# Decode attention with a DMA-bound cache stream: three more visits per layer turn with K as the moving operand, and loads into aligned slots

## The chip, the cores and the metric

One core of a Trainium2 chip. The metric is device time in microseconds (us) of the program, lower is better. The kernel before was measured at 2340.02 us (median of 3 runs, 2339.74 to 2343.99) when the prediction was made. The record sorts runs into a fast and a slow state by time and clock. Experiments 1 to 3 and the larger dose of experiment 4 ran on one chip, the others on a second one, each with runs of the kernel before in the same rounds.

Words used below. A *unit* is 512 KB of the K or V cache: 128 partitions, 4 KB each. A *visit* is the attention of one pair of heads of one batch row in one layer: four units of K, then four of V. *Batch row* b has 16 visits in layer 0 and 16 in layer 1. A *turn* is the place where the stream of visits goes from layer 0 to layer 1 of a row. There are eight. In the views, PE is TensorE's matmuls, PEld its weight loads, DVE is VectorE, ACT ScalarE, POOL GpSimd and SP SyncE, which issues the loads. In the traces each load of the cache has 16 completion records, and it *lands* when the last of them arrives. That each record stands for another of the 16 DMA engines of the page is my reading: the records do not name the engine.

## The reference, cut to what matters

```python
# B=8, Sq=1, D=640, 32 heads of 128, Sk=4096, Dff=1728; bf16
def _A_ref(x, k_cache, v_cache, wq, wo):
    q = (x @ wq) per head
    p = softmax(q @ k^T * Dh**-0.5)
    return (p @ v, heads joined) @ wo
x = x + _A_ref(_layernorm(x), A_k_cache, A_v_cache, A_wq, A_wo)
x = x + _B_ref(_layernorm(x), B_w1, B_w2)          # relu feed-forward
x = x + _A_ref(_layernorm(x), A_k_cache, A_v_cache, A_wq, A_wo)   # the same caches again
x = x + _B_ref(_layernorm(x), B_w1, B_w2)
```

Both layers read the same caches, 512 MB in all. What layer 1 can find on the chip need not be loaded again.

## The kernel before

A planner in Python writes one list of operations, and each engine gets its part in that order. The cache goes through an *arena* of 26 unit slots. At the end of layer 0 of a row, 21 slots keep units for layer 1 (three more wait outside the arena, in PSUM but for half a unit), so that only five slots take turns while the turn runs (the prediction's "24 of the 26" counts those three in):

```python
G = 26
SPARE = 5
...
keep = set(first[: G - SPARE])
stash = first[G - SPARE : G - SPARE + STASH]
```

Two visits of the next row ("ahead") are put in front of the first layer-1 visit, so that the feed-forward, the norm and the queries of the turn have something to hide behind. The visits that matter, with t the first visit of layer 1: t-3 is the last of layer 0, t-2 and t-1 are the two ahead.

K scores are formed in one of two ways. With K *still*, 16 blocks of 128x128 of a unit are loaded as weights and the query is one moving column. With K *moving*, the unit moves as four matmuls of 512 columns, and the score row must be turned again afterwards (PT, copied by PC):

```python
moving = [not any(t - AHEAD - 1 <= i < t + 5 for t in turns) and i < NV - 2 for i in range(NV)]
...
    for c in range(4):
        if moving[i]:
            nc.tensor.matmul(
                s_ps[32 * c : 32 * c + CJ, :], lhsT=qz[:, i % 3, c // 2, 3 - g : 3 - g + CJ],
                rhs=arena[:, at + c * BANK : at + (c + 1) * BANK], ...)
            continue
        ...
        for n in range(4 * c, 4 * c + 4):
            nc.tensor.matmul(s_tiles[i][:, j : j + 1], lhsT=arena[:, at + n * P : at + (n + 1) * P],
                             rhs=qo[:, b, h : h + 1], start=True, stop=True)
```

A load takes n neighbouring free units, up to 8, and goes where the slots have been free longest:

```python
def room(n):
    us = [u for u in range(G - n + 1) if not any(owner[u : u + n])]
    return min(us, key=lambda u: max(freed[u : u + n])) if us else None
```

In the turn the plan is a ring: consume a unit, release its slot, load one unit into it. For the second turn of the kernel before it reads (K-2.0 is unit 0 of K of visit t-2; `[ld1]` a load of one unit; T, M2, B, E are the steps of the softmax, C those of the feed-forward):

```
K-1.3 [ld1] M1 -1; C down 1; L -2; I -2
V-2.0 [ld1] C down 2; T -1; M2 -1
V-2.1 [ld1] C down 3; B -1; E -1
V-2.2 [ld1] C down 4; C add
V-2.3 [ld1] OC -2; L -1; I -1; C mean; C center
```

## Time and profile before

| | before |
|---|---|
| time | 2340.02 us |
| load queue, share of 16 DMA engines' span | 99.4% |
| PE busy | 60% |
| rate between turns, in turns (stretches of 20 us) | about 432, 370 to 415 GB/s |

From the page of the kernel before: its span, the rates in 40 slices, the load queue and the instruction fetches (packets, MB, share of 16 engines), and the chain of what ended last, by engine.

```profile
span 2343.0 us, 43024 instructions
...
GB/s 411 430 433 401 433 432 432 431 396 432 432 432 430 404 434 431 430 427 403 433 432 431 426 412 434 430 432 420 427 431 427 432 416 430 431 431 431 396 433 329
...
q1 hardware_dynamic: 76564, 988.12, 99.4%
q8 instruction: 146, 2.39, 0.4%
...
DMA 71%; PE 17%; ACT 6%; DVE 3%; issue 2%; SPq 0%; POOL 0%; ACTq 0%; DVEq 0%; POOLq 0%
```

The load queue is busy for the whole span. The rate stands near 430 except for a dip in every fifth slice or so: 401, 396, 404, 403, 412, 420, 416, 396. Those are the eight turns.

The groups of instructions that the change touches (line, engine, operation, out<-in, shapes, count; busy us, mean ns of one; idle before it and what ended that):

```profile
L695 PE MATMUL s_ps<-arena,qz 128*4 128x512 bf16 x3040 | 410.3, 602 | 261.1 <-DMA arena<-in_A_kv_dram 249.5
L713 DVE TENSOR_REDUCE mrow<-s_ps 100x1 bf16<-100x512 f32 x190 | 131.8, 694 | 323.2 <-PE s_ps L695 323.2
...
L705 PE MATMUL s_ps<-qo,arena 128*128 128x1 bf16 x3712 | 123.7, 165 | 17.2 <-ACT P_sb L761 7.6
L768 PE MATMUL small_ps<-few,P_row 100*128 100x16 bf16 x760 | 52.3, 179 | 92.1 <-ACT P_row L755 92.1
```

L695 is K moving, L705 K still. L713 (the maximum over the row, 0.69 us) and L768 (the turning of the row) exist for moving visits.

The loads of the cache, from the list of DMA issues (count, KB each, median us from issue to landing):

```profile
arena<-in_A_kv_dram SPq DMA_DIRECT2D x124, 4096.0 KB, 23.1
arena<-in_A_kv_dram SPq DMA_DIRECT2D x98, 2048.0 KB, 22.7
arena<-in_A_kv_dram SPq DMA_DIRECT2D x218, 512.0 KB, 6.5
arena<-in_A_kv_dram SPq DMA_DIRECT2D x48, 1024.0 KB, 11.3
```

The second turn in the view of stretches (start:end, us; busy us and count of PE, PEld, DVE, ACT, POOL; granted clock, DMA share, GB/s):

```profile
480.00:500.00 20.00, 15.92 (x385) 12.39 (x383) 4.91 (x29) 2.50 (x10) 2.33 (x11) 1.00 0.97 368
500.00:520.00 20.00, 16.16 (x341) 10.76 (x338) 5.18 (x30) 4.38 (x14) 2.54 (x12) 1.00 1.02 401
```

And PE in the timeline of the same turn (start us, length us, what; in brackets the idle time before it and what ended it). L687 are the V units, L580 is the down product of the feed-forward:

```profile
499.23 0.59 PE L687 MATMUL o_ps<-arena,P_sb 128*4 128x512 bf16 x4
499.76 0.62 PE L580 MATMUL small_ps<-hT,w_sb 128*128 128x1 bf16 x14
500.45 0.60 PE L687 MATMUL o_ps<-arena,P_sb 128*4 128x512 bf16 x4
500.99 0.23 PE L781 MATMUL s_ps<-P_sb,few 128*128 128x64 bf16 x1
501.53 0.19 PE L492 MATMUL s_ps<-s1h,few 128*128 128x1 bf16 x2 [0.32 <-DVE lsum L787]
501.74 0.59 PE L687 MATMUL o_ps<-arena,P_sb 128*4 128x512 bf16 x4
```

The V units follow each other at 499.23, 500.45 and 501.74: one per 1.2 to 1.3 us, the pace at which units land.

### The profile page before, as it was taken

How to read it: one execution, taken by the hardware profiler on the slowest of the kernel's cores; microseconds unless marked ns; L12 is line 12 of the kernel's file. 1: busy time of each engine (PE TensorE's matmuls, PEld its weight loads, DVE VectorE, ACT ScalarE, POOL GpSimd, SP SyncE). 2: the span in 40 equal slices, each digit the busy share in tenths (PEclk: the TensorE clock that was granted, in tenths of full speed). 3: DMA queues.
4: the chain of work that ended last, by engine and by line, in shares of the span. 5: the costliest groups of instructions: out<-in, count | busy, mean ns of one | idle time of the engine just before them, and what ended most of it. 6: DMA issues, size and time to landing. Idle time of an engine off the chain costs nothing.

```text
span 2343.0 us, 43024 instructions
## 1 busy us (share of the span) xinstructions
PE 1398.6 (60%) x18748; PEld 591.4 (25%) x18748; DVE 496.7 (21%) x2022; ACT 426.3 (18%) x986; POOL 59.5 (3%) x296
## 2 busy tenths in 40 slices
PE   3547654576545764557545675556755567545766
PEld 1214211152111511125111241113411133111523
DVE  1113211131112211122111221112211122111312
ACT  1111211122111221112211121111211112111211
POOL 0000000000000000000000000000000000000000
PEclk9999999999999998555555555555555555555555
DMA  9999999999999999999999999999999999999997
GB/s 411 430 433 401 433 432 432 431 396 432 432 432 430 404 434 431 430 427 403 433 432 431 426 412 434 430 432 420 427 431 427 432 416 430 431 431 431 396 433 329
DMA packets 76753, 990.87 MB, mean 423 GB/s; under 512 B 8596, under 2 KB 8596, under 8 KB 36500
## 3 DMA queue, kind: packets, MB, share of 16 engines
q1 hardware_dynamic: 76564, 988.12, 99.4%
q8 instruction: 146, 2.39, 0.4%
q14 instruction: 43, 0.35, 0.0%
HBM read 988.08 MB, written 0.01 MB: 422 GB/s over the span
## 4 chain that ended last, share of the span: by engine, by line
DMA 71%; PE 17%; ACT 6%; DVE 3%; issue 2%; SPq 0%; POOL 0%; ACTq 0%; DVEq 0%; POOLq 0%
DMA arena<-in_A_kv_dram 71%; PE o_ps L687 5%; PE s_ps L695 4%; PE s_ps L705 2%; ACT P_row L755 2%; ACT o_sb L795 1%; PE small_ps L655 1%; DVE mrow L713 1%; ACT P_sb L761 1%; PE small_ps L800 1%; ACT arena L634 1%; PE small_ps L768 1%; PE small_ps L825 1%; DVE hmx L732 0%; ACT nmax L753 0%
## 5 line engine op out<-in xcount | busy, mean ns | idle before, releaser
L687 PE MATMUL o_ps<-arena,P_sb 128*4 128x512 bf16 x3952 | 584.3, 596 | 402.0 <-DMA arena<-in_A_kv_dram 401.0
L695 PE MATMUL s_ps<-arena,qz 128*4 128x512 bf16 x3040 | 410.3, 602 | 261.1 <-DMA arena<-in_A_kv_dram 249.5
L687 PEld LDWEIGHTS <-P_sb 128*4 128x4 bf16 x3952 | 107.4, 88 | 502.8 <-issue 491.7
L713 DVE TENSOR_REDUCE mrow<-s_ps 100x1 bf16<-100x512 f32 x190 | 131.8, 694 | 323.2 <-PE s_ps L695 323.2
L795 ACT CAST o_sb<-o_ps 100x512 bf16<-100x512 f32 x247 | 144.9, 587 | 289.3 <-PE o_ps L687 286.0
L753 ACT ACTIVATE nmax<-small_ps 100x1 f32<-100x1 f32 x106 | 18.1, 171 | 774.5 <-PE small_ps L742 774.5
L775 DVE CAST P_sb<-small_ps 128x64 bf16<-128x64 f32 x190 | 42.6, 224 | 523.1 <-PE small_ps L768 523.1
L695 PEld LDWEIGHTS <-qz 128*4 128x4 bf16 x3040 | 63.9, 85 | 313.7 <-issue 295.5
L705 PEld LDWEIGHTS <-arena 128*128 128x128 bf16 x4224 | 129.6, 104 | 40.8 <-DMA arena<-in_A_kv_dram 23.4
L705 PE MATMUL s_ps<-qo,arena 128*128 128x1 bf16 x3712 | 123.7, 165 | 17.2 <-ACT P_sb L761 7.6
L768 PE MATMUL small_ps<-few,P_row 100*128 100x16 bf16 x760 | 52.3, 179 | 92.1 <-ACT P_row L755 92.1
L753 ACT ACTIVATE nmax<-small_ps,q_scale 100x1 f32<-100x1 f32 x84 | 22.0, 261 | 398.7 <-PE small_ps L742 398.7
L787 DVE TENSOR_REDUCE lsum<-small_ps 128x2 f32<-128x64 f32 x240 | 53.9, 224 | 171.9 <-PE small_ps L781 171.9
L768 PEld LDWEIGHTS <-P_row 100*128 100x128 bf16 x760 | 35.0, 107 | 186.5 <-ACT P_row L755 178.2
L720 PE MATMUL small_ps<-few,mrow 100*1 100x16 bf16 x190 | 34.4, 181 | 67.6 <-DVE mrow L713 67.6
L755 ACT ACTIVATE P_row<-s_ps,nmax 100x512 bf16<-100x512 f32 x106 | 72.8, 687 | 3.4
L800 PEld LDWEIGHTS <-o_sb 100*128 100x128 bf16 x988 | 45.7, 106 | 107.2 <-ACT o_sb L795 73.8
L655 PE MATMUL small_ps<-xq,wq_sb 128*128 128x1 bf16 x1200 | 48.8, 165 | 38.9 <-DVE qo L812 33.5
L800 PE MATMUL small_ps<-few,o_sb 100*128 100x2 bf16 x988 | 65.1, 170 | 10.7 <-DVE lsum L787 2.2
L727 DVE TENSOR_REDUCE diag<-small_ps 1x2 bf16<-1x16 f32 x190 | 30.8, 162 | 186.9 <-PE small_ps L720 186.9
L720 PEld LDWEIGHTS <-mrow 100*1 100x1 bf16 x190 | 15.0, 79 | 210.8 <-DVE mrow L713 210.8
L755 ACT ACTIVATE P_row<-s_ps,nmax,q_scale 100x512 bf16<-100x512 f32 x84 | 65.3, 778 | 2.8
(225 smaller groups left out, 958.0 us busy)
## 6 DMA issues: line engine op xcount, KB each, us to landing
arena<-in_A_kv_dram SPq DMA_DIRECT2D x124, 4096.0 KB, 23.1
arena<-in_A_kv_dram SPq DMA_DIRECT2D x98, 2048.0 KB, 22.7
arena<-in_A_kv_dram SPq DMA_DIRECT2D x218, 512.0 KB, 6.5
arena<-in_A_kv_dram SPq DMA_DIRECT2D x48, 1024.0 KB, 11.3
arena<-in_A_kv_dram SPq DMA_DIRECT2D x11, 3072.0 KB, 22.4
arena<-in_A_kv_dram SPq DMA_DIRECT2D x11, 2560.0 KB, 20.5
arena<-in_A_kv_dram SPq DMA_DIRECT2D x10, 1536.0 KB, 19.7
wq_sb<-in_A_wq_dram SPq DMA_DIRECT2D x4, 1280.0 KB, 17.6
```

The source lines that it names most:

```text
L655: nc.tensor.matmul(q_ps[:, h : h + 1], lhsT=wq_sb[:, g, c, (2 * n + h) * Dh : (2 * n + h + 1) * Dh], rhs=xlns[b][:, 0, c : c + 1], start=( ...
L687: nc.tensor.matmul(o_ps[32 * c : 32 * c + CJ, :], lhsT=P_tiles[i][:, h, j : j + CJ], rhs=arena[:, at + c * CJ * Dh : at + (c + 1) * CJ * D ...
L695: nc.tensor.matmul(s_ps[32 * c : 32 * c + CJ, :], lhsT=qz[:, i % 3, c // 2, 3 - g : 3 - g + CJ], rhs=arena[:, at + c * BANK : at + (c + 1) ...
L705: nc.tensor.matmul(s_tiles[i][:, j : j + 1], lhsT=arena[:, at + n * P : at + (n + 1) * P], rhs=qo[:, b, h : h + 1], start=True, stop=True,)
L713: nc.vector.tensor_reduce(out=m_tiles[i][:OR, :1], in_=s_ps[:OR], axis=AX.X, op=ALU.max)
L720: nc.tensor.matmul(turn_ps[:1, : 4 * CJ], lhsT=m[:OR, :1], rhs=rsel[:OR], start=True, stop=True)
L755: nc.scalar.activation(out=P_rows[i][:OR], in_=s_ps[:OR], func=ACT.Exp, bias=nm[:OR, :1], scale=more)
L768: nc.tensor.matmul(P_ps[:, k * 4 * CJ : (k + 1) * 4 * CJ], lhsT=P_row[:OR, k * P : (k + 1) * P], rhs=rsel[:OR], start=True, stop=True,)
L775: nc.vector.tensor_copy(out=P_tiles[i].rearrange("p h (c k) -> p h c k", k=BANK // P), in_=P_ps.rearrange("p (k h c) -> p h c k", k=BANK / ...
L787: nc.vector.tensor_reduce(out=L, in_=(lsum2_ps if ahead[i] else lsum_ps).rearrange("p (h j) -> p h j", h=2), axis=AX.X, op=ALU.add)
L795: nc.scalar.copy(out=o_tiles[i][:OR], in_=o_ps[:OR, :].rearrange("p (j d) -> p j d", j=CJ))
L800: nc.tensor.matmul(oy[i][:, :2], lhsT=o_tiles[i][:OR, j, :], rhs=gsel[:OR, j, :], start=(j == 0), stop=(j == CJ - 1))
```

## The change

Its intent: treat the visit in front of the ahead visits (t-3) and both ahead visits as moving, as most others are: 24 visits more, 214 of 256 in place of 190, which drops 2064 PE instructions. The first one ahead gets its score rows in the bank of the output, which therefore starts at -1e30, and the two columns that the last layer-0 visit writes must be cleared first. Besides, loads of more than 4 units start, where such a place is free, at slots divisible by 8, of 3 or 4 at slots divisible by 4, and small ones fill blocks already broken. The core of the diff:

```diff
-    moving = [not any(t - AHEAD - 1 <= i < t + 5 for t in turns) and i < NV - 2 for i in range(NV)]
+    moving = [not any(t <= i < t + 5 for t in turns) and i < NV - 2 for i in range(NV)]
 ...
     def room(n):
         us = [u for u in range(G - n + 1) if not any(owner[u : u + n])]
-        return min(us, key=lambda u: max(freed[u : u + n])) if us else None
+        step = 8 if n > 4 else 4 if n > 2 else n
+        def cost(u):
+            block = owner[u // 8 * 8 : u // 8 * 8 + 8]
+            return u % step, -sum(block) if n <= 2 else 0, max(freed[u : u + n])
+        return min(us, key=cost) if us else None
 ...
-            if i and (moving[i] or moving[i - 1]):
+            if i and not ahead[i] and (moving[i] or moving[i - 1]):
                 until(("E", i - 1))
 ...
                 ops.append(("O", i))
+                if i < NV - 1:
+                    ops.append(("clear", True))
 ...
-    nc.vector.memset(o_ps, 0.0)
+    nc.vector.memset(o_ps, -1e30)
 ...
+    def row_scores(i):
+        return o_ps if ahead[i] == AHEAD else s_ps
 # s_ps becomes row_scores(i) in the matmul, the maximum and the exponential of a moving visit;
 # the sums of ahead visits go to the common lsum_ps
```

More of the change, by code (lines that the diff above doesn't have):

```diff
@@ L239, in plan @@
             pad(i)
-            if i and (moving[i] or moving[i - 1]):
+            if i and not ahead[i] and (moving[i] or moving[i - 1]):
                 until(("E", i - 1))
             if moving[i] and not moving[i - 1]:
-                ops.append(("clear",))
+                ops.append(("clear", False))
         else:
@@ L414 @@
     P_ps = small_ps[:, 440 : 440 + 2 * NJ]
-    lsum2_ps = s_ps[:, 4 * NJ : 6 * NJ]
     mean2_ps, var2_ps, q2_ps = (s_ps[:, 6 * NJ + lo : 6 * NJ + hi] for lo, hi in ((0, 1), (1, 2), (2, 4)))
@@ L667, in do_qz, with do_clear @@
         nc.gpsimd.tensor_copy(out=qz[:, i % 3, :, 3], in_=qo[:, b, 2 * hp : 2 * hp + 2])
-    def do_clear():
-        nc.vector.memset(s_ps[:, : 8 * NJ], -1e30)
+    def do_clear(outputs):
+        for t in o2_ps if outputs else (s_ps[:, : 8 * NJ],):
+            nc.vector.memset(t, -1e30)
+    def row_scores(i):
+        return o_ps if ahead[i] == AHEAD else s_ps
     def do_mm(which, i, g, u):
@@ L695, in do_mm @@
                 nc.tensor.matmul(
-                    s_ps[32 * c : 32 * c + CJ, :], lhsT=qz[:, i % 3, c // 2, 3 - g : 3 - g + CJ],
+                    row_scores(i)[32 * c : 32 * c + CJ, :], lhsT=qz[:, i % 3, c // 2, 3 - g : 3 - g + CJ],
                     rhs=arena[:, at + c * BANK : at + (c + 1) * BANK],
@@ L700, in do_mm @@
                 continue
-            s_tiles[i] = o_ps[:, 2 * NJ : 4 * NJ] if ahead[i] == AHEAD else s_ps[:, i % 2 * 2 * NJ : (i % 2 + 1) * 2 * NJ]
+            s_tiles[i] = s_ps[:, i % 2 * 2 * NJ : (i % 2 + 1) * 2 * NJ]
             h = 2 * hp + c // 2
@@ L712, in do_m1 @@
         if moving[i]:
-            nc.vector.tensor_reduce(out=m_tiles[i][:OR, :1], in_=s_ps[:OR], axis=AX.X, op=ALU.max)
+            nc.vector.tensor_reduce(out=m_tiles[i][:OR, :1], in_=row_scores(i)[:OR], axis=AX.X, op=ALU.max)
             return
@@ L754, in do_e @@
             P_rows[i] = sm.tile([P, BANK], BF16, name="P_row", tag="row", bufs=1)
-            nc.scalar.activation(out=P_rows[i][:OR], in_=s_ps[:OR], func=ACT.Exp, bias=nm[:OR, :1], scale=more)
+            nc.scalar.activation(out=P_rows[i][:OR], in_=row_scores(i)[:OR], func=ACT.Exp, bias=nm[:OR, :1], scale=more)
             return
@@ L781, in do_l @@
         nc.tensor.matmul(
-            lsum2_ps if ahead[i] else lsum_ps, lhsT=ones_p, rhs=P_tiles[i].rearrange("p h j -> p (h j)"), start=True, stop=True
+            lsum_ps, lhsT=ones_p, rhs=P_tiles[i].rearrange("p h j -> p (h j)"), start=True, stop=True
         )
@@ L787, in do_i @@
         nc.vector.tensor_reduce(
-            out=L, in_=(lsum2_ps if ahead[i] else lsum_ps).rearrange("p (h j) -> p h j", h=2), axis=AX.X, op=ALU.add
+            out=L, in_=lsum_ps.rearrange("p (h j) -> p h j", h=2), axis=AX.X, op=ALU.add
         )
```

## The prediction

> What bounds the kernel: its DMA traffic, almost without gaps. The page gives the load queue 99.4% of the 16 engines' span of 2343.0 us; the chain of waits is 71% DMA, 17% PE. PE is 60% busy. From 2331 us on nothing loads (the stretches view: DMA share 0.02): a tail of 12 us that the change does not touch.
>
> The rate dips from 432 to about 370-400 GB/s in eight stretches, the turns from layer 0 to layer 1. There 24 of the 26 arena units are held and five take turns, so loads are single units: 218 loads of 512 KB (list of DMA issues). Two things cost there. Size: in the packet records a 4 KB row takes 159 ns (412 GB/s), a 16 KB row 611 ns (429), a 32 KB row 1213 ns (432). Starvation: the 4 KB packets average 167 ns against a median of 159, about 13 us per engine in sum. But the 16 completions of one load are spread over 3.5 to 5 us before a turn and 2 us after it, and the last of them still comes every 1.25 us all through the turn. So the engines that starve are those ahead of the slowest, which never stops; a faster PE recovers little of the dip.
>
> What the change does. Bytes are the same: 1856 units. By the order of the two programs:
> 1. Three visits per turn (24 in all) take K as the moving operand: per unit 4 matmuls of 512 columns (0.53-0.60 us) for 16 weight loads and 16 one-column matmuls (0.43-0.59 us). PE loses 2064 of 37498 instructions. Per visit DVE's maximum grows from 0.24 to 0.70 us, and a transposition (0.28 us on PE, 0.22 on DVE) comes in: more PE work and chain, not less.
> 2. A clear of two columns stands between the direct output and the first visit ahead: an estimated 0.3 us more wait for PE per turn.
> 3. Aligned slots: 4 MB loads go from 124 to 142, 2 MB from 98 to 70, 1 MB from 48 to 38; 512 KB stay (219).
>
> On the critical path. (1) and (2) sit on PE, which has slack in the turn: a single-unit load lands 5.5 us after issue, by my estimate 2 us of it queueing, so half a microsecond of PE delay is absorbed: 0. (3) With the packet medians the new mix needs 1.8 us less of every engine. Instructions: the fetch queue has 146 packets of 16 KB, 933 ns each. [...] 37498/146 = 257 PE instructions per packet. So 8 packets fewer: 0.5 us as a mean over engines, perhaps 2 us on the one that lags. Sum: 2 to 4 us, 0.15%.
>
> Prediction: 2336.5 us, range 2329 to 2341.5. Faster by over 2%: 0.02; within 2%: 0.96; slower: 0.02.
>
> Right if: the load queue's share stays at 99%; the eight dips remain, with 26-27 single-unit loads each; fetch packets fall to about 138; the one-column K group loses 24 visits; the tail stays near 12 us.
>
> Wrong if: the lagging engine does starve in the turns, so that PE's delay or relief shows one for one (up to 2.5 us per turn, 20 us in all); waiting for four or eight aligned free units starves the queue after a turn (slower); or fetches fall mostly on the lagging engine (8 us faster).

The sum: 0 for (1) and (2), 1.8 us for (3), 0.5 to 2 us for the fetches, 2 to 4 us together. That a single-unit load queues for 2 us, and that the fetches save perhaps 2 us on the engine that lags, are my estimates; no record gave them.

## More of the kernel before

A *ring* is the small set of slots that take turns while the others are held.

Between turns a load lands some 23 us after its issue: a deep queue. The single-unit loads of the ring land after 6.5 us: a shallow one.

## The result

The changed kernel takes 2344.84 us (median of 6 runs, 2342.08 to 2347.38), against 2341.22 us (6 runs, 2339.27 to 2344.88) for the kernel before. The ratio is 1.0013, 95% interval 1.0000 to 1.0025. Ratios here are the mean time of one kernel's fast runs over that of the other's of the same rounds, so not quite the ratio of the medians. By the interval the loss is between 0 and 6 us. The time lies outside the predicted range (2329 to 2341.5), on the slow side: some 3 us were lost where 2 to 4 had been expected as a gain.

The same parts of the profile after, in the same order. The page:

```profile
span 2343.8 us, 41029 instructions
...
GB/s 410 429 433 391 433 430 433 431 384 431 431 434 430 406 433 431 433 427 410 435 431 432 426 412 432 433 429 423 415 431 431 433 415 425 431 433 429 399 433 338
...
q1 hardware_dynamic: 73252, 988.12, 99.4%
q8 instruction: 138, 2.26, 0.3%
```

(The chain of the changed kernel adds up to 16% in the page: its way back was lost early, so it says nothing.) Bytes are equal, fetch packets fell from 146 to 138, and the dips are there. Two are deeper by 10 or more, 391 for 401 and 384 for 396: the first two turns. The other six differ by 7 at most, both ways. (The two profiled runs are only 0.8 us apart; the one of before was among the slower ones of its kernel.) The groups:

```profile
L707 PE MATMUL s_ps<-arena,qz 128*4 128x512 bf16 x3296 | 443.9, 601 | 201.7 <-DMA arena<-in_A_kv_dram 188.9
...
L725 DVE TENSOR_REDUCE mrow<-s_ps 100x1 bf16<-100x512 f32 x206 | 142.9, 694 | 303.0 <-PE s_ps L707 303.0
...
L780 PE MATMUL small_ps<-few,P_row 100*128 100x16 bf16 x856 | 59.0, 179 | 104.2 <-ACT P_row L767 104.2
...
L717 PE MATMUL s_ps<-qo,arena 128*128 128x1 bf16 x2688 | 86.8, 165 | 10.1 <-ACT P_sb L773 7.6
```

From the groups with forms kept apart, the scores that now go to the output bank:

```profile
L707 PE MATMUL o_ps<-arena,qz 128*4 128x512 bf16 x128 | 19.1, 586 | 3.5 <-DVE o_ps L680 2.5 <-DVE s_ps L680 0.4
```

The clear costs PE 2.5 us in 8 turns, 0.3 us each, as the prediction had estimated. The loads:

```profile
arena<-in_A_kv_dram SPq DMA_DIRECT2D x142, 4096.0 KB, 23.2
arena<-in_A_kv_dram SPq DMA_DIRECT2D x70, 2048.0 KB, 19.7
arena<-in_A_kv_dram SPq DMA_DIRECT2D x219, 512.0 KB, 6.4
arena<-in_A_kv_dram SPq DMA_DIRECT2D x38, 1024.0 KB, 9.6
```

The second turn in stretches:

```profile
480.00:500.00 20.00, 16.02 (x284) 9.46 (x281) 6.57 (x33) 2.30 (x5) 2.31 (x11) 0.50 0.97 375
500.00:520.00 20.00, 16.14 (x338) 10.76 (x339) 4.96 (x29) 5.24 (x16) 2.52 (x12) 0.50 0.97 356
```

In this turn, the one with the largest loss of the eight, the loss is in the second half: 356 GB/s where there were 401. The granted clock also differs (0.50 and 1.00), but runs of the changed kernel at a mean clock of 0.76 and 0.56 took 2346.32 and 2342.08 us, so a higher clock did not visibly buy time here. PE at that place:

```profile
500.63 0.59 PE L699 MATMUL o_ps<-arena,P_sb 128*4 128x512 bf16 x4
501.67 0.28 PE L780 MATMUL small_ps<-few,P_row 100*128 100x16 bf16 x4 [0.45 <-ACT P_row L767]
502.33 0.60 PE L588 MATMUL small_ps<-hT,w_sb 128*128 128x1 bf16 x14 [0.38 <-DVE P_sb L787]
502.87 0.60 PE L699 MATMUL o_ps<-arena,P_sb 128*4 128x512 bf16 x4
503.39 0.23 PE L793 MATMUL small_ps<-P_sb,few 128*128 128x64 bf16 x1
503.71 0.36 PE L500 MATMUL s_ps<-s1h,few 128*128 128x1 bf16 x2
504.20 0.60 PE L699 MATMUL o_ps<-arena,P_sb 128*4 128x512 bf16 x4
```

Between the V units at 500.63 and 502.87 PE now stands still twice: 0.45 us for the exponential of the score row, which PT turns, and 0.38 us for VectorE's copy of the turned row, before the feed-forward piece. The unit consumed at 502.87 had landed at 501.80 by its completion record. Its slot was therefore released a good microsecond late.

### The profile page after: what moved, and what is told of

Its sections match the earlier page's. It is cut to its first block, busy times and chain, and to the rows that moved or that the text cites. A ratio compares the mean times of both kernels' runs of the same rounds, so it can differ in the third digit from the quotient of the medians.

```text
span 2343.8 us, 41029 instructions
## 1 busy us (share of the span) xinstructions
PE 1403.5 (60%) x17716; PEld 568.0 (24%) x17716; DVE 507.4 (22%) x2038; ACT 431.8 (18%) x962; POOL 63.2 (3%) x318
## 3 DMA queue, kind: packets, MB, share of 16 engines
q1 hardware_dynamic: 73252, 988.12, 99.4%
## 5 line engine op out<-in xcount | busy, mean ns | idle before, releaser
L699 PE MATMUL o_ps<-arena,P_sb 128*4 128x512 bf16 x3952 | 576.5, 595 | 470.0 <-DMA arena<-in_A_kv_dram 469.1
L707 PE MATMUL s_ps<-arena,qz 128*4 128x512 bf16 x3296 | 443.9, 601 | 201.7 <-DMA arena<-in_A_kv_dram 188.9
L725 DVE TENSOR_REDUCE mrow<-s_ps 100x1 bf16<-100x512 f32 x206 | 142.9, 694 | 303.0 <-PE s_ps L707 303.0
L707 PEld LDWEIGHTS <-qz 128*4 128x4 bf16 x3424 | 74.2, 85 | 262.5 <-issue 241.2
L780 PE MATMUL small_ps<-few,P_row 100*128 100x16 bf16 x856 | 59.0, 179 | 104.2 <-ACT P_row L767 104.2
L717 PE MATMUL s_ps<-qo,arena 128*128 128x1 bf16 x2688 | 86.8, 165 | 10.1 <-ACT P_sb L773 7.6
L717 PEld LDWEIGHTS <-arena 128*128 128x128 bf16 x2688 | 81.0, 104 | 14.9 <-issue 13.7
L767 ACT ACTIVATE P_row<-s_ps,nmax 100x512 bf16<-100x512 f32 x121 | 83.2, 687 | 3.9
L675 POOL COPY qz<-qo 128x2 bf16<-128x2 bf16 x128 | 23.9, 192 | 1864.6 <-PE s_ps L707 1718.3
L732 PE MATMUL small_ps<-few,mrow 100*1 100x16 bf16 x214 | 40.4, 189 | 54.2 <-DVE mrow L725 54.2
```

The source lines that it names most:

```text
L699: nc.tensor.matmul(o_ps[32 * c : 32 * c + CJ, :], lhsT=P_tiles[i][:, h, j : j + CJ], rhs=arena[:, at + c * CJ * Dh : at + (c + 1) * CJ * D ...
L707: nc.tensor.matmul(row_scores(i)[32 * c : 32 * c + CJ, :], lhsT=qz[:, i % 3, c // 2, 3 - g : 3 - g + CJ], rhs=arena[:, at + c * BANK : at ...
L725: nc.vector.tensor_reduce(out=m_tiles[i][:OR, :1], in_=row_scores(i)[:OR], axis=AX.X, op=ALU.max)
L767: nc.scalar.activation(out=P_rows[i][:OR], in_=row_scores(i)[:OR], func=ACT.Exp, bias=nm[:OR, :1], scale=more)
L780: nc.tensor.matmul(P_ps[:, k * 4 * CJ : (k + 1) * 4 * CJ], lhsT=P_row[:OR, k * P : (k + 1) * P], rhs=rsel[:OR], start=True, stop=True,)
```

## The experiments

Two theories and chance. **T1**: in the ring of five slots a delay of PE is paid in DMA time, and the moving ahead visits bring such a delay. **T2**: the choice of aligned groups of free slots starves the queue. **T3**: the difference is noise.

For several of them I add up the DMA records of the profiled run. *Nominal* is every load packet at the median duration of its size, over 16 engines. *Fetch* is the instruction packets' time over 16. *Rest* is what is left of the stretch from the first load packet to the mean completion of the last load: starvation and stretched packets, as a mean over engines. By its making it follows the time whatever took it, so it sorts the time and does not show a cause. One profiled run each; the rest moves by a few us from run to run, as the times do.

| run | span | nominal | fetch | rest |
|---|---|---|---|---|
| before | 2343.0 | 2310.8 | 8.5 | 8.6 |
| after | 2343.8 | 2309.0 | 8.1 | 12.9 |
| aligned slots only | 2338.6 | 2309.0 | 8.5 | 6.6 |
| moving visits only | 2346.3 | 2310.8 | 8.1 | 12.6 |
| turning (PT) later | 2340.0 | 2309.0 | 8.1 | 8.5 |
| dose of 5 | 2356.4 | 2310.8 | 8.8 | 22.3 |
| dose of 2 | 2349.5 | 2310.8 | 8.7 | 15.6 |
| front visit only | 2335.7 | 2309.0 | 8.4 | 4.2 |
| control (experiment 5) | 2340.8 | 2310.8 | 8.8 | 6.4 |
| six slots | 2343.2 | 2318.9 | 8.5 | 2.1 |
| six slots, dose of 5 | 2356.3 | 2318.9 | 8.8 | 14.6 |

A second sum looks at the turns alone: the *excess*, by which the gaps between last completions exceed 1.213 us per unit, from 5 us before a turn's first single-unit issue to 10 us after its last one, over all eight turns (us). Some 13 us of it are the size of the single-unit packets (8 of 159 ns for each 1213 ns); "elsewhere" is the same sum over the rest of the run.

| run | excess in the turns | elsewhere |
|---|---|---|
| before | 25.6 | 16.8 |
| aligned slots only | 25.2 | 13.0 |
| front visit only | 20.7 | 14.3 |
| control (experiment 5) | 22.1 | 18.4 |
| after | 26.8 | 16.6 |
| moving visits only | 28.1 | 17.6 |
| turning (PT) later | 24.3 | 15.1 |
| dose of 2 | 34.0 | 15.3 |
| dose of 5 | 41.7 | 14.2 |
| six slots | 16.5 | 17.0 |
| six slots, dose of 5 | 29.5 | 17.2 |

The first four rows have no added work in the ring and differ by 5 us among themselves: the doses stand out of that scatter, the change itself does not.

### 1 and 2: the two parts of the change apart

Edit of the first: the new `room` in the kernel before. Edit of the second: the old `room` in the changed kernel. The load sizes follow `room` alone, so the split is clean.

```diff
 # e1_align_only: before, with
-        return min(us, key=lambda u: max(freed[u : u + n])) if us else None
+        ... (step and cost(u) of the change)
+        return min(us, key=cost) if us else None
 # e2_moving_only: after, with the reverse of that
```

> The kernel before with the aligned choice of slots alone; the visits keep K still. Theory T1 (the loss is PE delay in the ring of five single-unit slots, brought by the moving visits): faster than before by the 1.8 us that the packet medians give, ratio 0.9992 (0.998 to 1.000), and the gaps between last landings in the turns look like those of before (sum of excess over 1.213 us per unit near 25 us). Theory T2 (waiting for four or eight aligned free units starves the queue): slower than before, ratio 1.001 or more, with gaps after the turns. T3 (the difference is chance): ratio 1.000.

Measured: 2340.26 us (5 runs, 2339.12 to 2340.61) against 2341.54 for before, ratio 0.9994 (0.9982 to 1.0007).

> The changed kernel with the slots of before: only the three visits per turn are moving. T1: slower than before by the change's loss plus what alignment gave, 3 to 6 us, ratio 1.0015 to 1.0025, and in the second half of the ring (around the second visit ahead, its V) gaps of 1.6 to 2.3 us between last landings in several turns. T2: as fast as before, or faster by a few tenths of a us for 8 instruction fetches fewer. T3: 1.000.

Measured: 2344.76 us (2342.59 to 2348.19), ratio 1.0016 (1.0002 to 1.0030).

The aligned slots give about what the packet sizes say (1.8 us of nominal time; the interval holds 1 too) and starve nothing: the excess in the turns is 25.2 us against 25.6, near the 25 expected. T2 falls. The moving visits cost what the change lost. Their interval leaves out 1 only just, so T3 is unlikely rather than excluded by this run alone; but of the runs of the same rounds, all five with moving visits (2342.59 us and more) were slower than all five with aligned slots (2340.61 and less). The trace of the moving visits alone has the same two waits of PE at the same place of the second turn, 0.46 and 0.38 us. In the rest column, moving raises it from 8.6 to 12.6 and aligning does not raise it.

### 3: the same change, with the turning one place later

```diff
-        for c in sorted(now, key=lambda c: len(c) > 1 and not c[1][0]):
+        for c in sorted(now, key=lambda c: (len(c) > 1 and not c[1][0], bool(c[0][1]) and c[0][1][0] == "PT")):
```

> The changed kernel, with one order changed: in a step the transposition of a moving visit's row (PT) is issued on PE after the other layer's feed-forward piece, not before it. In the trace of after PE stood still 0.45 us for the row and 0.38 us for the copy at this place, and three units behind it were released 1.1 us late. T1: most of this delay goes, the landing gaps of 1.6 to 1.9 us in the second half of the ring go, and the time falls by 1 to 5 us below after, ratio to before 0.9990 to 1.0005. T2 and T3: no change against after, ratio 1.001.

Measured: 2341.69 us (2340.87 to 2342.11), ratio 1.0001 (0.9989 to 1.0014). The slowest of these five runs, 2342.11, is level with the fastest of the changed kernel, 2342.08; the moving visits alone, in the same rounds, began at 2342.59. The ratios of this run and of the changed kernel come from different rounds, and their intervals overlap. PE in its timeline, at the place shown above:

```profile
500.56 0.59 PE L699 MATMUL o_ps<-arena,P_sb 128*4 128x512 bf16 x4
501.09 0.62 PE L588 MATMUL small_ps<-hT,w_sb 128*128 128x1 bf16 x14
502.13 0.26 PE L780 MATMUL small_ps<-few,P_row 100*128 100x16 bf16 x4 [0.42 <-DVE xT L596]
502.32 0.60 PE L699 MATMUL o_ps<-arena,P_sb 128*4 128x512 bf16 x4
```

The feed-forward piece now runs while the exponential does, and the V units are 1.76 us apart (500.56, 502.32) instead of 2.24. By the medians, an order of two operations on one engine is worth about 3 us of a DMA-bound kernel. That is T1, with one wait of 0.42 us still in place. Part of the cost stays: this run is 1.4 us slower than aligned slots alone by the medians. And the expected end of the long landing gaps came only in part: one of 1.61 us is left in the late ring of the second turn, whose excess fell from 5.5 to 4.5 us.

### 4: PE delay by the dose

The delay itself, without moving visits: in the kernel before, the last down piece of each turn is done again, with the same result.

```diff
         finishing[layer, b][op](*args)
+        if layer == 0 and op == "down" and args[0] == DC - 1:
+            for _ in range(5):          # 2 in the smaller dose
+                finishing[layer, b][op](*args)
```

> The kernel before, with the last piece of the feed-forward down product of each turn done six times in place of once (same result, about 0.55 us of PE each, so 2.8 us more PE at one place in the ring, in 7 turns). If the slack of the ring is 2 us, as the prediction assumed: 0.8 us per turn, 6 us in all, ratio 1.0025. If it is 0.6 us, as the landings of after suggest (a load that waits for nothing lands 4.9 us after issue, five units last 6.2 us): 2.2 us per turn, 15 us in all, ratio 1.0065. If the engine that lags covers everything: 1.000.

Measured: 2359.94 us (2358.17 to 2361.06), ratio 1.0079 (1.0067 to 1.0092). By the medians that is 18.4 us, or 2.3 us in each of eight turns (the expectation says seven; it was eight). The dose in its timeline:

```profile
499.75 3.39 PE L580 MATMUL small_ps<-hT,w_sb 128*128 128x1 bf16 x84
503.06 0.60 PE L690 MATMUL o_ps<-arena,P_sb 128*4 128x512 bf16 x4
```

3.39 us where before had 0.62: 2.8 us more, of which 2.3 are paid. With the 2 us of slack that the prediction had assumed, only 0.8 would have been paid.

> The kernel before with the last down piece of a turn done three times in place of once, 1.1 us more PE at that place in each of 8 turns. With the slack that six times gave (18.4 us / 8 = 2.3 us paid of 2.75, slack 0.45): 0.65 us per turn, 5.2 us in all, ratio 1.0022. With no slack at all: 8.8 us, 1.0038. With 2 us of slack: 1.000.

Measured: 2350.51 us (2347.79 to 2351.31), before 2340.71 (9 runs), ratio 1.0037 (1.0024 to 1.0051). Twice the piece is about 1.1 us per turn, 8.8 us in all, and the ratio gives 8.7. My slack of 0.45 us, read off the larger dose, was a miss: with it the ratio had been 1.0022, below the interval. A small delay is paid about whole (by the interval, 5.6 to 11.9 of 8.8 us). The excess in the turns says where: it rises by 8 us with the dose of 2 and by 16 with the dose of 5, and elsewhere it does not rise.

### 5: a control, the same dose where the queue is deep

```diff
-        for c in range(DC):
+        for c in list(range(DC)) * (10 if layer == 0 and hp == 8 else 1):
             for h in range(2):
                 nc.tensor.matmul(oy[i][:, ...], lhsT=wo_sb[...], ...)
```

> A control: the kernel before with about 2.6 us more PE per batch, the same size as the larger dose, but at the ninth visit of layer 0, where loads land some 20 us after issue: the output product of that visit is done ten times in place of once (same result). T1 (PE delay is paid in the ring alone): no change, ratio 1.000 (0.999 to 1.001). If more PE work costs wherever it stands: 18 to 20 us, 1.008.

The product in its timeline, before the second turn; at the other visits there it takes 0.43 us (10 matmuls):

```profile
430.39 2.83 PE L825 MATMUL small_ps<-oT,wo_sb 128*128 128x1 bf16 x100
```

Measured: 2341.70 us (2339.77 to 2342.85), before 2341.05 (10 runs), ratio 1.0003 (0.9989 to 1.0016). So 2.4 us more of the same engine (2.6 had been expected) cost nothing detectable in the middle of layer 0. The cost belongs to the ring, not to PE's work. Nor is it the instruction fetches: this control has 152 of them, the dose of 5 has 151, the kernel before 146.

### 6: one slot more

```diff
-SPARE = 5
+SPARE = 6
```

> The kernel before with six turning slots in place of five (one unit fewer is kept, so 8 units more are loaded: 8 times 1.21 us = 9.7 us) and the down piece six times. T1: one slot more is 1.21 us more slack, so the dose costs 8 times (2.75 - 1.7) = 8.4 us in place of 18.4: ratio (9.7 + 8.4) / 2341 = 1.0077. If the slack has nothing to do with the number of slots: 9.7 + 18.4 = 28 us, 1.012.

> The kernel before with six turning slots and no dose, the pair of the run with six slots and the dose. It loads 8 units more, 8.1 us by the packet medians. If the ring of five costs the kernel before nothing, the ratio is 1.0035; what it comes out below that, the ring of five had cost. Against this run the dose should have cost less than the 18.4 us that it cost with five slots: with 19.8 us for both, 11 to 14 us.

Measured: with the dose 2360.50 us (4 runs, 2358.08 to 2362.92), ratio 1.0084 (1.0070 to 1.0098). Without it 2344.75 us (6 runs, 2344.24 to 2346.66), ratio 1.0018 (1.0005 to 1.0030).

The first expectation came out nearly right by two errors that cancel. Six slots alone cost about 4 us, not 9.7 or the 8.1 of nominal time: the sixth slot gave some 4 us back (1 to 7 by the interval), so the ring of five had cost the kernel before about that much even without a dose. And the dose with six slots costs 15.7 us (2360.50 less 2344.75), not 8.4, nor the 11 to 14 of the second expectation. A slot more is not 1.21 us more slack. What it may be, the completion records suggest, below.

### 7: only the visit in front, and a version that beats both

The kernel before with aligned slots and the moving visit in front of the ahead visits, which runs before the ring:

```diff
-    moving = [not any(t - AHEAD - 1 <= i < t + 5 for t in turns) and i < NV - 2 for i in range(NV)]
+    moving = [not any(t - AHEAD <= i < t + 5 for t in turns) and i < NV - 2 for i in range(NV)]
 # e6 also: sums over the output weights, once in the program
-            if i == NP - 2:
+            if i == NP - 4:
                 ops.append(("WS", closing))
```

> Aligned slots, and of the three visits per turn only the one in front of the ahead visits is moving; the two ahead, which run inside the ring of five slots, keep K still as before. T1 (the cost lies in the ring alone): as aligned slots alone, ratio 0.9994 (0.998 to 1.0005), and few gaps over 1.4 us between last landings late in the ring. If the moving visits cost wherever they stand: a third of 3.5 us more, ratio 1.000 or above.

Measured: 2338.90 us (2337.51 to 2341.67), before 2340.71, ratio 0.9993 (0.9980 to 1.0005), the same as aligned slots alone (0.9994). A moving visit outside the ring costs nothing that shows; the loss is with the two ahead visits inside it.

> The same, with the sums over the output weights (two reductions of 1.39 and 1.50 us with their copies, 3.7 us of VectorE in all, once, in the first turn, on the chain from 192.99 to 196.70 us of before) done two visits earlier, ahead of the ring. T1 says that a delay in the ring over about half a microsecond is paid: 1 to 2.5 us faster than the run beside it, ratio to before 0.9985 to 0.9990, and the first turn's excess falls from 4.5 to 2.5 us. If the ring absorbs it: no change.

The second edit takes another delay out of the ring of the first turn. In the chain of waits of before it stood there as two long pieces (start us, length us, what):

```profile
192.99 1.39 DVE wsum L479
...
194.81 1.50 DVE wsum L479
```

Measured: 2337.42 us (2334.72 to 2339.69), ratio 0.9985 (0.9972 to 0.9997). This version beats both kernels: about 3 us under the kernel before, with an interval that leaves out 1, and about 6 us under the changed one by ratios (0.9985 against 1.0013, from different rounds). Against the version beside it the step of 1.5 us is as large as expected, but the two intervals overlap. In the first turn the excess was 4.8 us in the version beside it and 3.2 here; single turns differ by as much between runs, so this supports the step and does not show it.

## Why the prediction was wrong

**Right: what bounds the kernel and what does not change.** The load queue's share is 99.4% again (it tells little: the dose of 5, 18 us slower, still has 99.1%: its 4 KB packets average 170 ns where before had 167, and all of that counts as busy), the dips remain with 219 single-unit loads, the tail is within 0.2 us by the last completion (10.6 and 10.4 us). One-column score matmuls lost 24 visits: 3712 in the group shown, and 512 in the output bank, became 2688 and none.

**Right: the size terms.** Nominal time fell by 1.8 us, as predicted from the packet medians, and aligned slots alone agreed with it (1.3 us by the medians). Fetches fell from 146 to 138 and by 0.4 us as a mean. Divided by the fetch packets (16 KB each: 146 of them are 2.39 MB), the PE and PEld instructions of the two pages give the same before and after: 37496/146 and 35432/138 are both 257 per packet.

**Wrong: the step "(1) and (2) sit on PE, which has slack in the turn ... so half a microsecond of PE delay is absorbed: 0".** It measured 3 to 4 us instead of 0 (moving visits only, 1.0016 of 2341; by the interval 0.5 to 7). What came true is the prediction's own first "wrong if", that PE's delay shows one for one. Doses of 1.1 and 2.8 us per turn were paid at about 100% and 83%. I had taken 2 us of the 5.5 us from issue to landing for queueing that a late issue could eat up, without a record that showed a load landing faster in the ring. The dosed run has one such load, below: issued late, it landed 4.5 us after its issue instead of 5.5. So the last engine had about 1 us to give, and the delay was paid all the same. The delay was also larger than the half microsecond: at the place shown PE waited 0.83 us, and the unit that had landed at 501.80 was used at 502.87.

**Wrong: the inference beneath it, "the engines that starve are those ahead of the slowest, which never stops; a faster PE recovers little of the dip".** The observation held roughly (the excess of before is 3.2 us per turn), and the conclusion did not follow. The first and the last of the 16 completions of one load are 0.9 to 5.3 us apart in the run of before. PE used a unit only after the last of them: in that trace 229 starts of matmuls or weight loads that had waited over 0.2 us for a load came 0.04 us after its last completion. Its slot comes free later still, and by then, as I read it, the engines in front have only what the ring has issued. In the second turn, from the completion records (issue of a load; first and last of its 16 completions; spread; gap to the last completion of the load before):

```
kernel    issue    first    last     spread  gap
before    499.87   503.07   505.37   2.30    1.27
before    501.10   504.86   506.60   1.74    1.23
before    502.38   506.38   507.93   1.55    1.33
after     501.27   504.35   506.76   2.42    1.28
after     503.50   506.49   508.37   1.89    1.61
after     504.84   508.10   510.23   2.13    1.86
dose of 5 499.86   503.90   506.83   2.93    1.23
dose of 5 503.70   506.57   508.18   1.61    1.35
dose of 5 505.04   508.18   509.46   1.28    1.28
dose of 5 506.02   509.63   510.94   1.31    1.48
```

In the dosed run one issue comes 3.84 us after the one before it, and the last completion hardly notices at first: a gap of 1.35 us. What gives way is the spread, from 2.93 to 1.28 us: as I read it, the engines in front have starved and lost their lead. I had called that free. But the last completions lose afterwards: over the eight turns their excess is 41.7 us where before had 25.6 (in this one turn it is 3.3 against 3.2; the others rise by 0.3 to 3.6). It would be free if one engine were the slowest for good. Following the sixteen completions from load to load between turns, it is not so. Here are they in order, in us after the first, of three loads 75 and 120 us apart, before the second turn:

```
last at 235.2: 0.00 0.10 0.24 0.25 0.29 0.31 0.50 0.59 0.63 0.90 1.02 1.05 1.24 1.64 1.95 2.40
last at 310.6: 0.00 0.04 0.23 0.24 0.27 1.00 1.14 1.59 1.70 1.78 1.94 2.00 2.17 2.20 2.27 3.75
last at 430.9: 0.00 0.04 0.25 0.32 0.79 1.52 1.62 1.79 1.98 2.05 2.13 2.56 3.02 3.24 3.78 5.30
```

Around eight of the ten instruction fetches between the first and the last of these lines, one place in the row moves back by 1.5 to 1.6 us (2.42 became 3.93 at the one at 246.4 us, 3.78 became 5.30 at 425.3 us); around the other two, at 304.8 and 327.5 us, two places move, by 0.7 to 1.7 us. The place changes: most of the row has moved by the third line. So the fetches seem to fall on changing engines, and the lead of an engine would be what pays for the next fetch that falls on it. When the ring starves the engines in front, that credit is lost, and fetches that follow in the turn would show in the gaps. The time would then be the mean engine's work plus the mean engine's starvation. This fits the sixth slot too: with it the spread in the ring of the dosed run is 3.2 to 3.8 us instead of 2.9. The engines in front would run further ahead, to the end of the ring again, and a late issue would still starve them.

How far this is shown: that a delay in the ring is paid, and outside it is not, is measured. That it is paid in the last completions of the turns themselves is measured for the doses; for the change, 3 us are too few for one profiled run each. That the leads of the engines carry it is my reading of completion records and not shown: the records do not name the engine, so the rotation is followed by order, not by name, and no run removes the fetches. Why the rate stays at 240 to 290 GB/s for four microseconds after the dose (504 to 508 us of its run; from 500 to 520 us it has 376 where before had 401), while later loads are already issued, is open.

## What to carry to other kernels

In a DMA-bound kernel, ask at each place how deep the load queue is before calling another engine's delay free: some 2.4 us of PE cost nothing detectable where loads land 23 us after issue, and 2.8 us cost 2.3 where five single-unit slots take turns. Fewer instructions is not the aim in such a place; the time from a unit's landing to its slot's release is, and a wait for another engine in front of the next unit could here be moved by swapping two operations (about 3 us by the medians). Do not reason from the slowest of 16 DMA engines alone: here the dose left the next last completion almost alone (a gap of 1.35 us), and was paid, over eight turns, in those that followed (an excess of 41.7 us where before had 25.6).
